# Linear attention with decay and a maxout layer: decay sums for one token of a pair, wider relus, another written order

## The chip, the cores and the metric

The kernel runs on one core of a Trainium2 chip. The metric is the device time of one execution in microseconds; a time given for a kernel is the median of its runs. Engines are named as the profile names them: PE is TensorE (PEld its weight loads), DVE is VectorE, ACT is ScalarE, POOL is GpSimd, SP is SyncE, which issues the DMAs.

## The reference

```python
# attention: q, k, v, alpha are (4, 8, 768, 48) = batch, heads, tokens, width; alpha in 0.8 .. 1.0
for t in range(S):
    state = alpha[:, :, t, :, None] * state + np.einsum('bhd,bhe->bhde', k[:, :, t], v[:, :, t])
    y[:, :, t] = np.einsum('bhd,bhde->bhe', q[:, :, t], state)
# x = y as (3072 tokens, 384); w1, w2 are (384, 1024), w_out is (1024, 384)
h1, h2 = x @ w1, x @ w2
out = np.maximum(h1, h2) @ w_out
```

Everything comes and goes as float32.

## The kernel before, in words

**The maths.** The decay recurrence is done in chunks. With L the running sum of log alpha inside a chunk, a query is multiplied by exp(L), a key by exp(-L), and inside the chunk the outputs are a masked score matrix times the values; the state (48 by 48 a head) is carried from chunk to chunk. The maxout layer is rewritten as max(h1, h2) = h2 + relu(h1 - h2): the kernel forms wd = w1 - w2 and m = w2 times w_out once, and then computes relu(x wd) w_out + x m.

**The tiling.** The tokens of a batch are cut into three blocks of 256, so there are twelve blocks n = 0 to 11, each with all eight heads. A partition holds a pair of neighbouring tokens j = 0, 1; 128 pairs make a block, and its two halves of 64 pairs are its chunks, x = 0, 1. Blocks 0 and 1 do their first steps in two halves of four heads, the others do all eight at once. Each block gives two strips of 128 output tokens, and the maxout layer takes these two strips as one group g of W = 256 tokens.

**The steps of a block** (names as in the order below, with lines of the kernel before):
- `lda`, `ldk`, `ldq`, `ldv` (L452): loads of alpha, k, q, v. One buffer of a ring of ten holds a and k, another q and v; each half of a weight matrix takes one too (`ldw1`, `ldw2`, `ldwo`).
- `ln` (L591, ACT): log of alpha, as float16. `su` (L599, DVE): the sum of the two logs of a pair.
- `cs` (PE): the decay sums. For each group of four heads one matmul of 384 columns with the constant `cmat` (L610) gives the sum up to and with the pair, written for both tokens; one of 192 columns with the negated identity (L613) takes the second token's log off again for the first token. Four small ones (L618) give the sums per head that the state needs. The result fills two PSUM banks.
- `en`, `ep` (L628, L632, ACT): exp(-sum) and exp(sum) of 768 elements. `gg` (L637): the same of the small sums.
- `kt` (L648) and `qt` (L654): key times exp(-L) and query times exp(L), float16. `vc` (L664, POOL): values to float16.
- `tk`, `tq` (L681, PE) and `ck`, `cq` (copies): transposes of keys and queries, in blocks 0 to 7. Blocks 8 to 11 transpose by DMA (`dk`, `dq`, L721).
- `kv` (L741, PE): key times value. `w` (DVE), `t32` and `T` (L788, L776, mostly POOL): the state carried on, and its float16 copy for the outputs. `g` (L754): a product of decays.
- `sc` (L821, PE): scores. `pt` (L829, DVE): scores times the mask. `yf`, `y` (L866, PE): the outputs, from state and scores. `xe`: the outputs to float16.

**The steps of a group**: `h` (L931): for each of the eight column blocks f of 128, three matmuls of 256 columns into a PSUM bank. `r` (L939 on DVE, L941 on ACT): one relu of 256 columns per f. `o` (L964): the output of a strip, eleven matmuls of 384 columns in two parts, a and b. `ev` and `st` (L973): copy to SBUF and store. `wtp`, `wtc`, `woc`, `wd`, `mp`, `mc` prepare the weights, `fill` are matmuls on zeros (L423) that keep PE busy at the start.

**What sets the order.** A planner class could choose an order from costs, but a written order (`ORDER`) stands in its place: a list of words `step:engine`, with the PSUM bank behind P. The instructions are emitted in this sequence, and each engine, SP's queue too, works off its own instructions in that sequence; a waiting instruction holds all behind it on its engine. The relevant helper reads:

```python
for word in ORDER.split():
    name, at = word.split(":")
    o = ops[name]
    o.eng = eng[at[0]]
```

Of the kernel before, what the change touches and what calls it, by code (L numbers as in the profile page):

```python
# [24 lines left out]
class Op:  # L25
    __slots__ = ("name", "engs", "emit", "deps", "takes", "uses", "prio", "mode", "xfer", "eng", "start", "end", "seen", "n", "after", "until", "port", "k")
# [5 lines left out]
GROUPS = (2, 2, 2, 2, 2, 2, 2, 2, 2, 2, 2, 2)  # L32
# [7 lines left out]
setp1:G fz:D lda0.0:S setd0:D fill0:P7 lda0.1:S fill12:P ldw21:S fill32:P fill31:P ldk0.0:S fill34:P pads1:D ldq0.0:S fill9:P ln0.0:A id32:D fill15:P  # L40
su0.0:D fill11:P ln0.1:A setd1:D ldv0.0:S fill16:P fill21:P su0.1:D mask:D cs0.0:P0 cs0.1:P ldw20:S gg0.0:A fill28:P en0.0:A pads0:D wtp1.2:P6 en0.1:A
fill8:P gg0.1:A wtp1.0:P5 ep0.0:A kt0.1:D ep0.1:A lda1.0:S fill6:P fill13:P kt0.0:G wtc1.2:A wtp1.1:P4 lda1.1:S fill3:P qt0.0:D fill14:P ldwo0:S
fill27:P tk0.0:P2 qt0.1:D tk0.1:P fill22:P ck0.0:A tq0.0:P fill36:P tq0.1:P vc0.1:G cq0.0:A fill29:P fill2:P cq0.1:D vc0.0:G fill4:P ck0.1:A ldw10:S
fill10:P wtc1.0:D pads2:G sc0.0:P0 kv0:P2 pt0.0:D fill19:P wtp0.1:P6 w0:D ldwo1:S wtp0.0:P5 ln1.0:A wtc0.1:D su1.0:D fill24:P ln1.1:A t32.1:D fill17:P
sc0.1:P0 su1.1:D fill23:P w1:D T1.0:G fill30:P wtp0.2:P6 pt0.1:D ldw11:S T1.1:G cs1.0:P2 woc0.0:G fill1:P wtc0.2:D gg1.0:A y0:P0 en1.0:A wtc0.0:D
woc0.1:A ldk1.0:S cs1.1:P mp0.1:P6 gg1.1:A wd0.0:D wtc1.1:A mp0.2:P5 ldq1.0:S xe1:A wd0.1:D mp0.0:P4 xe0:A fill7:P h0.0:P1 woc1.1:A woc1.0:D ldv1.0:S
fill20:P fill26:P g1:G fill5:P en1.1:A T2.1:G mp1.1:P ep1.0:A mp1.2:P lda2.0:S r0.0:A wd1.1:D mc1:A h0.1:P0 fill25:P h0.3:P6 wd1.0:D h0.6:P7 r0.3:A
h0.2:P1 r0.1:A mp1.0:P mc2:D kt1.0:G r0.2:A lda3.0:S h0.5:P6 r0.6:D mc0:A h0.4:P5 ldq2.0:S kt1.1:G tk1.0:P0 ep1.1:A qt1.0:D h0.7:P7 r0.4:A ck1.0:D
tq1.0:P t32.2:G r0.5:A tk1.1:P qt1.1:D o0.1a:P5 ldk2.0:S r0.7:A cq1.0:D vc1.0:G ck1.1:A tq1.1:P sc1.0:P2 vc1.1:G cq1.1:D T2.0:G kv1:P6 ldk3.0:S
o0.1b:P ln2.0:A w2:D pt1.0:D T3.1:G T3.0:G o0.0a:P4 ldv2.0:S ev0.1:A t32.3:D yf1:P0 ln3.0:A su2.0:D sc1.1:P2 o0.0b:P w3:D pt1.1:D ldq3.0:S cs2.0:P6  # L50
ev0.0:A su3.0:D y1:P lda4.0:S en2.0:A cs3.0:P2 kt2.0:G xe2:A xe3:D st0.1:S ep2.0:A h1.0:P5 st0.0:S h1.1:P4 r1.0:D gg3.0:A h1.4:P1 gg2.0:A qt2.0:D
r1.1:A g2:G ldv3.0:S h1.3:P5 T4.0:G en3.0:A h1.5:P0 h1.2:P4 vc2.0:G r1.3:D tk2.0:P6 ep3.0:A r1.2:D ldq4.0:S h1.6:P5 kt3.0:G ck2.0:D tq2.0:P r1.5:A
h1.7:P4 r1.4:A qt3.0:D o1.0a:P0 r1.7:A ldv4.0:S r1.6:A o1.1a:P1 T4.1:G cq2.0:D ln4.0:A tk3.0:P2 t32.4:G kv2:P4 ldk4.0:S sc2.0:P6 ck3.0:A tq3.0:P w4:D
pt2.0:D T5.1:G o1.1b:P cq3.0:A T5.0:G lda6.0:S su4.0:D yf2:P4 sc2.1:P6 vc3.0:G ev1.1:A sc3.1:P2 o1.0b:P pt2.1:D ldq7.0:S pt3.1:D y2:P ev1.0:A lda5.0:S
sc3.0:P0 vc4.0:G cs4.0:P6 xe4:A xe5:D pt3.0:D h2.0:P5 ldq6.0:S kv3:P2 r2.0:A h2.6:P4 en4.0:A h2.5:P5 w6:D h2.1:P1 r2.6:D T7.1:G r2.5:A h2.2:P0
ldk6.0:S T7.0:G h2.4:P4 r2.1:A r2.2:D h2.7:P5 ep4.0:A t32.7:G h2.3:P1 o2.0a:P0 kt4.0:G w7:D gg4.0:A ldv6.0:S r2.3:A r2.4:D r2.7:A qt4.0:D y3:P2
ln6.0:A lda7.0:S g4:G kv4:P4 t32.8:G xe6:A o2.0b:P su6.0:D xe7:A w8:D tk4.0:P6 st1.1:S T9.0:G ev2.0:D h3.0:P1 T8.0:G ldk5.0:S tq4.0:P ck4.0:D r3.0:A
h3.5:P0 t32.9:G cs6.0:P2 cq4.0:D r3.5:A T9.1:G h3.4:P1 ldq5.0:S w9:D T8.1:G gg6.0:A h3.3:P0 en6.0:A r3.4:D h3.7:P7 sc4.0:P4 r3.3:D h3.6:P6 kt6.0:G
ep6.0:A pt4.0:D ldv5.0:S h3.2:P1 o2.1a:P0 ln5.0:A qt6.0:D r3.7:A h3.1:P5 vc6.0:G ldv7.0:S o2.1b:P r3.1:A r3.6:A su5.0:D yf4:P2 r3.2:D ev2.1:A sc4.1:P4
cs5.0:P6 ldk7.0:S ln7.0:A pt4.1:D o3.0a:P1 en5.0:A lda9.0:S y4:P ep5.0:A kt5.0:G kv6:P4 xe8:A o3.0b:P w12:D lda8.0:S xe9:A su7.0:D o3.1a:P0 ev3.0:A  # L60
qt5.0:D t32.13:G gg5.0:A h4.0:P1 g5:G t32.10:G ldk8.0:S cs7.0:P2 w13:D r4.0:A T13.1:G h4.1:P7 en7.0:A h4.7:P6 T10.1:G h4.4:P1 r4.7:D tk5.0:P4 vc5.0:G
r4.1:A st3.0:S h4.3:P6 ep7.0:A ck5.0:D h4.5:P7 ldq9.0:S vc7.0:G o3.1b:P r4.5:A qt7.0:D T10.0:G gg7.0:A r4.4:A tq5.0:P kt7.0:G r4.3:A h4.6:P7 st2.0:S
cq5.0:D tk6.0:P2 ldq8.0:S h4.2:P6 ev3.1:D tq6.0:P r4.2:A ck6.0:D kv5:P4 g7:G sc5.0:P0 t32.14:G o4.0a:P6 r4.6:D cq6.0:A ldv8.0:S T13.0:G w10:D pt5.0:D
T11.0:G o4.1a:P7 ln9.0:A T11.1:G st1.0:S kv7:P2 ln8.0:A yf5:P0 ldv9.0:S sc5.1:P4 w14:D o4.0b:P pt5.1:D t32.15:G o4.1b:P ldk9.0:S w15:D y5:P su9.0:D
ev4.1:A su8.0:D ev4.0:D sc6.0:P2 tk7.0:P4 T15.0:G xe11:A xe10:D ldq10.0:S cs8.0:P6 T14.0:G ck7.0:A pt6.0:D h5.0:P1 vc8.0:G tq7.0:P r5.0:A h5.1:P0
lda10.0:S cq7.0:D en8.0:A h5.2:P3 h5.4:P2 r5.1:D h5.5:P1 kt8.0:G r5.4:A h5.6:P5 r5.5:D r5.2:A h5.7:P4 st2.1:S h5.3:P2 r5.6:D r5.7:A cs9.0:P0 r5.3:D
ep8.0:A sc6.1:P4 T14.1:G dk8:S o5.1a:P3 gg9.0:A qt8.0:D T15.1:G en9.0:A o5.0a:P2 lda11.0:S ep9.0:A pt6.1:D o5.1b:P gg8.0:A g8:G qt9.0:D t32.16:G
kv8:P4 ldk10.0:S ev5.1:A y6:P6 w16:D sc7.0:P0 o5.0b:P xe12:D T17.0:G xe13:A vc9.0:G pt7.0:D h6.0:P3 ev5.0:A yf7:P4 kt9.0:G sc7.1:P6 r6.0:A h6.1:P2
pt7.1:D h6.2:P3 r6.1:A h6.4:P1 ln10.0:A h6.3:P0 h6.7:P2 r6.4:D dk9:S kv9:P6 su10.0:D r6.7:A y7:P r6.2:D w18:D dq8:S cs10.0:P2 t32.19:G xe14:A xe15:D
h6.6:P1 T16.1:G r6.3:D h7.0:P5 st3.1:S w19:D r6.6:A h6.5:P4 r7.0:D en10.0:A h7.2:P0 st4.0:S h7.3:P1 h7.7:P5 r6.5:A o6.0a:P7 dq9:S r7.7:A ep10.0:A  # L70
h7.6:P6 h7.4:P5 ldv10.0:S ln11.0:A r7.6:D o6.1a:P4 r7.4:D st4.1:S gg10.0:A qt10.0:D g10:G h7.1:P6 T19.0:G h7.5:P5 r7.1:A o6.0b:P t32.20:G r7.5:D
T17.1:G r7.3:D o6.1b:P T16.0:G ev6.0:A r7.2:D kt10.0:G sc8.0:P0 ev6.1:D yf8:P2 sc8.1:P6 o7.1a:P5 pt8.1:D o7.0a:P4 T19.1:G dk10:S pt8.0:D o7.1b:P
st6.0:S su11.0:D y8:P ldk11.0:S vc10.0:G ev7.1:D ldq11.0:S sc9.0:P0 sc9.1:P6 T20.0:G xe16:D xe17:A o7.0b:P pt9.0:D h8.0:P5 dq10:S ev7.0:A cs11.0:P2
pt9.1:D r8.0:A h8.5:P4 h8.6:P5 h8.1:P1 r8.6:A h8.2:P0 r8.5:D r8.1:A kv10:P6 en11.0:A y9:P4 w20:D r8.2:D T21.1:G gg11.0:A h8.3:P1 t32.21:G xe19:D
xe18:A o8.1a:P0 kt11.0:G ep11.0:A w21:D h9.0:P7 r8.3:A h8.7:P6 h9.1:P5 r8.7:D h9.2:P4 T20.1:G r9.1:A dk11:S h9.4:P1 r9.2:D h9.7:P6 T21.0:G r9.4:A
h9.6:P5 qt11.0:D g11:G r9.7:A h8.4:P4 ldv11.0:S T22.1:G o8.0a:P1 r9.0:A r9.6:D st5.1:S r8.4:D sc10.0:P2 st5.0:S yf10:P6 sc10.1:P4 pt10.0:D o8.0b:P
o8.1b:P dq11:S pt10.1:D ev8.0:A h9.5:P1 h9.3:P3 st7.0:S o9.1a:P2 vc11.0:G st6.1:S ev8.1:A y10:P t32.22:G r9.3:A st8.1:S T22.0:G r9.5:A kv11:P4
o9.0a:P3 xe21:D xe20:A w22:D h10.0:P7 T23.0:G o9.0b:P T23.1:G r10.0:D sc11.0:P0 ev9.0:A yf11:P4 sc11.1:P6 pt11.0:D o9.1b:P st9.0:S st8.0:S h10.6:P3
pt11.1:D ev9.1:A h10.2:P1 h10.3:P0 r10.6:A st9.1:S h10.4:P2 h10.1:P3 st7.1:S r10.4:D y11:P r10.1:A r10.2:D o10.0a:P1 xe22:D xe23:A h11.0:P7 h10.5:P6
h10.7:P5 r10.5:D o10.1a:P4 r10.7:D r10.3:D h11.2:P6 o10.0b:P r11.2:A r11.0:A h11.5:P6 ev10.0:D h11.4:P7 h11.1:P5 h11.3:P3 r11.1:D h11.6:P2 h11.7:P1  # L80
r11.6:D o10.1b:P r11.7:A r11.3:D r11.5:D o11.1a:P5 ev10.1:A o11.0a:P6 r11.4:A st10.1:S o11.1b:P o11.0b:P ev11.1:A st11.1:S o11.1c:P7 ev11.0:D st10.0:S
o11.1d:P st11.0:S ev11.11:A st11.11:S
"""
SHIFT = {}
FIX = {}


class Plan:


    LAT = {"PE": 0.25, "ACT": 0.08, "DVE": 0.08, "POOL": 0.1, "SP": 0.0}
    SWITCH = 0.09
    LEAD = 4.5
# [51 lines left out]
    def give(self, b):  # L145
# [4 lines left out]
        else:  # L150
            self.free[b.pool][b.at] = True

    def add(self, name, engs, emit, deps=(), takes=(), uses=(), prio=0.0, mode=None, xfer=0.0, after=None, until=None, port=False, k=0):
        o = Op()
        o.k = 2 * k + 0.35 if k else 0
        o.until = until
        o.port = port
        prio += SHIFT.get(name, 0.0)
        if name in FIX:
            engs = {FIX[name]: engs[FIX[name]]}  # L160
# [867 lines left out]
```

## Time and profile before

| | |
|---|---|
| runs before | 143.17, 143.81, 142.78 us, median 143.17 |
| profiled execution | 142.84 us, its span 141.0 us |
| busy in the span, us | PE 133.4, PEld 96.1, DVE 92.5, ACT 74.9, POOL 65.1 |
| L610 and L613 (sums), count and mean ns | 24 of 328, 24 of 246 |
| L941 and L939 (relus of 256), count and mean ns | 55 of 383 on ACT, 41 of 419 on DVE |
| L648 (key product, 768 elements, POOL) | 10 of 1810 ns |
| loads of 384 KB, issue to landing | about 6 us |

The span is the part of the execution in which the profile sees the engines; 1.8 us of the profiled time lie outside it. Busy times of different engines overlap. A matmul's own duration holds its latency, so back-to-back matmuls overlap and the distance between their starts is what each one costs PE. The page cuts the span into 40 slices of 3.5 us and gives the busy tenths of each.

### The profile page before, as it was taken

The page shows a single profiled execution, that of the slowest core. Times are in us where ns is not written, and L with a number is a line of the kernel's source. Part 1 is how long each engine was busy: PE and PEld are TensorE (multiplying, and loading weights), DVE is VectorE, ACT ScalarE, POOL GpSimd, SP SyncE. Part 2 cuts the span into 40 slices and gives each one's busy share as a digit, 9 for nine tenths or more (in the row PEclk, how much of TensorE's full clock was granted, in tenths as well). Part 3 has the DMA queues.
Part 4 walks back from the last instruction along what each step waited for, and adds up shares of the span by engine and source line. Part 5 has one row for each costly group of instructions (what it writes and reads, how often), then busy time and mean ns, then how long its engine had stood idle before and what let it go on. Part 6 is the DMA issues. An engine that isn't in the chain of part 4 may idle for free.

```text
span 141.0 us, 5542 instructions
## 1 busy us (share of the span) xinstructions
PE 133.4 (95%) x2373; PEld 96.1 (68%) x2373; DVE 92.5 (66%) x186; ACT 74.9 (53%) x159; POOL 65.1 (46%) x108
## 2 busy tenths in 40 slices
PE   6779889989999999999999999999999999999991
PEld 2355666666877778767885976787667776777770
DVE  6615984679586976875596877873688476385420
ACT  3624267654977494876772783657205634241230
POOL 5036343652696287627994373721940742500000
PEclk9999999999999999999999999999999999999999
DMA  5999999999999999999999989397669359641014
GB/s 121 291 257 296 371 377 331 260 235 268 266 315 258 255 246 258 299 230 248 268 282 252 280 211 221 80 146 198 170 122 250 62 105 242 201 176 51 0 56 167
DMA packets 64680, 30.76 MB, mean 218 GB/s; under 512 B 58896, under 2 KB 63120, under 8 KB 64656
## 3 DMA queue, kind: packets, MB, share of 16 engines
q1 hardware_dynamic: 64656, 30.41, 85.8%
q8 instruction: 18, 0.29, 1.0%
q14 instruction: 6, 0.05, 0.1%
HBM read 23.59 MB, written 4.72 MB: 201 GB/s over the span
## 4 chain that ended last, share of the span: by engine, by line
PE 77%; SPq 10%; DMA 9%; DVE 1%; issue 1%; ACT 0%; DVEq 0%
PE PS L964 32%; PE PS L931 21%; PE PS L866 9%; DMA ldf<-in_q_dram 9%; SPq L452 6%; PE PS L681 5%; PE PS L821 4%; SPq L474 3%; PE PS L741 3%; PE PS L610 2%; SPq L471 2%; PE PS L613 1%; PE PS L618 1%; DVE xT L494 0%; DVE qkt L654 0%
## 5 line engine op out<-in xcount | busy, mean ns | idle before, releaser
L931 PE MATMUL PS<-xT,wd 128*128 128x256 f16 x288 | 37.8, 273 | 0.1
L964 PE MATMUL PS<-wo,g 128*128 128x384 f16 (+1 forms) x200 | 37.8, 320 | 0.0
L829 DVE TENSOR_TENSOR pt<-PS,mask 128x1024 f16<-128x1024 f32 x24 | 28.8, 1216 | 3.4 <-PE PS L821 3.4
L931 PEld LDWEIGHTS <-wd 128*128 128x128 f16 x288 | 26.8, 98 | 5.9 <-DVE w L801 0.4
L648 POOL TENSOR_TENSOR qkt<-ldf,en 128x768 f16<-128x768 f32 (+1 forms) x13 | 21.5, 1657 | 18.8 <-DMA ldf<-in_k_dram 10.0
L941 ACT ACTIVATE g<-PS 128x256 f16<-128x256 f32 x55 | 19.6, 383 | 16.2 <-PE PS L931 16.1
L964 PEld LDWEIGHTS <-g 128*128 128x128 f16 x200 | 18.7, 98 | 10.6
L939 DVE TENSOR_SCALAR g<-PS 128x256 f16<-128x256 f32 x41 | 16.3, 419 | 10.3 <-PE PS L931 9.5
L776 POOL TENSOR_TENSOR T<-w,gg 48x192 f16<-48x192 f32 x24 | 12.4, 518 | 12.7 <-DVE w L801 8.7
L492 ACT COPY outs<-PS 128x384 f32<-128x384 f32 (+1 forms) x18 | 8.3, 461 | 18.7 <-PE PS L964 17.2
L964 PE MATMUL PS<-m,xT 128*128 128x384 f16 (+1 forms) x75 | 15.9, 321 | 0.0
L492 ACT CAST xT<-PS 128x384 f16<-128x384 f32 x15 | 8.5, 595 | 12.1 <-PE PS L866 10.9
L664 POOL CAST v<-ldf 128x768 f16<-128x768 f32 (+1 forms) x14 | 10.2, 740 | 8.7 <-DMA ldf<-in_v_dram 8.5
L654 DVE TENSOR_TENSOR qkt<-ldf,PS 128x384 f16<-128x384 f32 x24 | 12.2, 547 | 2.5 <-DMA ldf<-in_q_dram 2.1
L423 PE MATMUL PS<-fz 128*128 128x512 f16 x34 | 11.7, 447 | 1.2 <-DVE fz L420 1.2
L591 ACT ACTIVATE loga<-ldf 128x768 f16<-128x768 f32 (+1 forms) x14 | 10.4, 750 | 4.4 <-DMA ldf<-in_alpha_dram 4.3
L681 PE MATMUL PS<-ident,qkt 128*128 128x128 f16 x128 | 10.2, 219 | 0.9 <-DVE qkt L654 0.7
L776 POOL TENSOR_TENSOR T<-w,g 48x192 f16<-48x192 f32 x16 | 8.6, 539 | 4.1 <-PE PS L866 3.5
L866 PE MATMUL PS<-pt,v 64*64 64x128 f16 x576 | 10.4, 218 | 0.0
L681 PEld LDWEIGHTS <-qkt 128*128 128x128 f16 x128 | 8.3, 98 | 2.9 <-DVE qkt L654 1.0
L628 ACT ACTIVATE en<-PS 128x768 f32<-128x768 f32 (+1 forms) x14 | 9.9, 715 | 0.4 <-POOL t L788 0.2
L632 ACT ACTIVATE PS<-PS 128x768 f32<-128x768 f32 (+1 forms) x14 | 10.0, 725 | 0.0
(73 smaller groups left out, 162.2 us busy)
## 6 DMA issues: line engine op xcount, KB each, us to landing
ldf<-in_k_dram SPq DMA_DIRECT2D x12, 384.0 KB, 6.0
ldf<-in_q_dram SPq DMA_DIRECT2D x12, 384.0 KB, 6.2
ldf<-in_v_dram SPq DMA_DIRECT2D x12, 384.0 KB, 6.0
out_dram<-outs SPq DMA_DIRECT2D x23, 192.0 KB, 3.5
ldf<-in_alpha_dram SPq DMA_DIRECT2D x10, 384.0 KB, 6.4
ldf<-in_moe_w_dram SPq DMA_DIRECT2D x4, 768.0 KB, 8.0
ldf<-in_moe_w_out_dram SPq DMA_DIRECT2D x2, 768.0 KB, 8.7
ldf<-in_alpha_dram SPq DMA_DIRECT2D x4, 192.0 KB, 4.5
```

Of the source, the lines that this page charges most:

```text
L423: plan.add(f"fill{i}", {"PE": 0.21}, lambda eng: nc.tensor.matmul(bank(fb), lhsT=fz[:, 0:128], rhs=fz, start=True, stop=True, skip_group_c ...
L492: nc.scalar.copy(out=out, in_=in_)
L648: e.tensor_mul(out=hjd(qkts[i3], 1)[:, hd], in0=A["ld", n, "k"][:, hd].rearrange("p h (j d) -> p h j d", j=2), in1=A["en", n][:, g0:g1].re ...
L654: nc.vector.tensor_mul(out=hjd(qkts[i3], 0)[:, 4 * g : 4 * g + 4], in0=A["ld", n, "q"].rearrange("p h (j d) -> p h j d", j=2)[:, 4 * g : 4 ...
L681: nc.tensor.transpose(t[:, a, r, j, :], src[:, j, r, :], ident16)
L776: e.tensor_mul(out=T16s[m % 4][o : o + 48, :, 48 * u : 48 * u + 48], in0=w_[o : o + 48], in1=g_[o : o + 48])
L829: nc.vector.tensor_mul(out=t.rearrange("p u r c -> p (u r) c"), in0=A["sc", n, hf].rearrange("p u (r c) -> p (u r) c", r=2), in1=mask.rear ...
L866: nc.tensor.matmul(dst, lhsT=lhsT, rhs=rhs, start=(x, u) not in begun, stop=done and ends[x, u] == i, skip_group_check=True)
L931: nc.tensor.matmul(t[:, 0:W], lhsT=wd16[:, s, f * 128 : (f + 1) * 128], rhs=xT[:, s, a0 : a0 + W], start=(s == 0), stop=(s == 2))
L939: nc.vector.tensor_relu(o, i)
L941: nc.scalar.activation(out=o, in_=i, func=ACTF.Relu)
L964: nc.tensor.matmul(A["op", t0, c], lhsT=lhsT, rhs=rhs, start=(part == 0 and j == 0), stop=(part == 1 and j + 1 == len(todo[1])))
```

## The change

- The sums are made for the second token of a pair only: one matmul of 384 columns with `cmat` per block, one PSUM bank. The negated identity is gone. `en` and `ep` take 384 elements, and `kt` and `qt` read them once for each token of the pair.
- The first token is put right beforehand: its key is multiplied by the second token's alpha (`ka`), its query by exp(-log alpha) of the second token (`inv` on ACT, then `qi`). Both work in place in the load buffer.
- Two column blocks f share a PSUM bank, and one relu takes 512 columns: 48 `h` steps of six matmuls, 48 `r` steps. The first part of an output takes three matmuls with x and four with g (three before), the second four (five before).
- `su`, `kt`, `vc`, `T` and `t32` may be put on other engines. In the new order: `su` 10 on POOL and 4 on DVE (14 on DVE before), full and half `kt` 7 on DVE and 7 on POOL (1 and 13), `vc` 11 on ACT and 3 on POOL (14 on POOL), `T` 10 on DVE and 30 on POOL (40 on POOL), `ka` 6 on DVE and 8 on POOL, `qi` 4 and 10, `fill` 41 (34).
- The written order is another one on every queue.

The core of the diff:

```diff
-                for g in gs:
-                    nc.tensor.matmul(t[:, g, 0:384], lhsT=cmat,
-                                     rhs=s16[:, 4 * g : 4 * g + 4, 0:D].unsqueeze(2).to_broadcast([128, 4, 2, D]),
-                                     start=True, stop=False, skip_group_check=True)
-                    nc.tensor.matmul(t[:, g, 0:384].rearrange("p (h j d) -> p h j d", h=4, j=2)[:, :, 0, :], lhsT=nid16,
-                                     rhs=l1[:, 4 * g : 4 * g + 4, :], start=False, stop=True, skip_group_check=True)
+                t, s16 = A["cs", n], s16s[i2]
+                nc.tensor.matmul(t[:, h0 * D : h1 * D].rearrange("p (h d) -> p h d", d=D), lhsT=cmat, rhs=s16[:, h0:h1, 0:D],
+                                 start=True, stop=True, skip_group_check=True)
...
+                nc.scalar.activation(out=A["inv", n][:, hd], in_=A["loga", n][:, hd, 1, :], func=ACTF.Exp, scale=-1.0)
...
+                kk = A["ld", n, "k"][:, hd, 0:D]
+                e.tensor_mul(out=kk, in0=kk, in1=A["ld", n, "a"][:, hd, D : 2 * D])
...
+                qq = A["ld", n, "q"][:, hd, 0:D]
+                e.tensor_mul(out=qq, in0=qq, in1=A["inv", n][:, hd])
...
-            kt = plan.add(f"kt{n}.{i}", ke, e_kt, deps=[en, lk[0], pads[i3]] + free3, uses=[bk, enb], prio=Q + 6, port=True)
+            kt = plan.add(f"kt{n}.{i}", ke, e_kt, deps=[en, ka, lk[0], pads[i3]] + free3, uses=[bk, enb], prio=Q + 6, port=True)
...
-                t = A["h", g, f] = bank(ps, WMAX)
-                for s in range(3):
-                    nc.tensor.matmul(t[:, 0:W], lhsT=wd16[:, s, f * 128 : (f + 1) * 128], rhs=xT[:, s, a0 : a0 + W],
-                                     start=(s == 0), stop=(s == 2))
+                t = A["h", g, f] = bank(ps, 2 * W).rearrange("p (f w) -> p f w", f=2)
+                for i in range(2):
+                    for s in range(3):
+                        nc.tensor.matmul(t[:, i], lhsT=wd16[:, s, (f + i) * 128 : (f + i + 1) * 128], rhs=xT[:, s, a0 : a0 + W],
+                                         start=(s == 0), stop=(s == 2), skip_group_check=True)
...
-                o, i = A["g16", g][:, f, 0:W], A["h", g, f][:, 0:W]
+                o, i = A["g16", g][:, f : f + 2], A["h", g, f]
...
-                    todo = [gw[:4], xm + gw[4:]] if early else [xm + gw[:3], gw[3:]]
+                    todo = [gw[:4], xm + gw[4:]] if early else [xm + gw[:4], gw[4:]]
```

The stretch of the order around blocks 1 and 2 that the prediction walks through, the words of PE alone. Before:

```
h0.0 fill20 fill26 fill5 mp1.1 mp1.2 h0.1 fill25 h0.3 h0.6 h0.2 mp1.0 h0.5 h0.4 tk1.0 h0.7 tq1.0 tk1.1 o0.1a tq1.1 sc1.0 kv1 o0.1b o0.0a yf1 sc1.1 o0.0b cs2.0 y1 cs3.0 h1.0
```

After:

```
h0.0 mp1.1 mp1.2 mp1.0 h0.2 h0.4 h0.6 o0.0a tk1.0 o0.0b kv1 tk1.1 tq1.0 fill33 tq1.1 fill35 fill38 fill11 sc1.0 o0.1a yf1 sc1.1 cs2.0 o0.1b y1 cs3.0 tk2.0 h1.0
```

The loads on SP's queue, before: a0, half of w2, k0, q0, v0, half of w2, a1, half of wo, half of w1, the other halves of wo and w1, k1, q1, v1, a2, a3, q2, k2, k3, v2, q3, a4. After: a0, half of w2, half of a1, k0, q0, the rest of a1, half of w2, v0, half of wo, half of w1, the other halves of wo and w1, q1, k1, v1, a2, k2, a3, q2, q3, k3, v2, v3, a4. The planner's costs for the new steps and engines, which the written order leaves unused, are left out here.

## The prediction

> **What bounds the kernel now.** I read the page first, for which engine is full and when.
>
> ```profile
> PE 133.4 (95%) x2373; PEld 96.1 (68%) x2373; DVE 92.5 (66%) x186; ACT 74.9 (53%) x159; POOL 65.1 (46%) x108
> ...
> PE   6779889989999999999999999999999999999991
> ```
>
> TensorE has holes in the first ten slices (35 us) only. PE's waits name them all, and they add up to 4.5 us:
>
> ```profile
> PE PS L511 <- DMA ldf<-in_moe_w_dram: 2.0, 2, 1.6
> PE PS L423 <- DVE fz L420: 1.2, 1, 1.2
> PE PS L681 <- DVE qkt L654: 0.7, 1, 0.7
> PE PS L866 <- DVE pt L829: 0.4, 1, 0.4
> PE PS L681 <- POOL qkt L648: 0.2, 1, 0.2
> ```
>
> Then the chain of waits from 28 us on (start, length, what), because a busy PE need not be at its rate.
>
> ```profile
> 15.68 12.45 DMA ldf<-in_q_dram
> ...
> 28.83 0.71 PE PS L681 x8
> ...
> 34.66 0.16 PE PS L610
> 34.82 0.08 PE PS L613
> 34.91 0.16 PE PS L610
> 35.07 0.08 PE PS L613
> 35.15 0.08 PE PS L618 x4
> ...
> 36.93 2.16 PE PS L931 x18
> ...
> 58.06 0.35 PE PS L821 x16
> ...
> 61.57 0.22 PE PS L821 x16
> ...
> 133.65 4.43 PE PS L964 x38
> 138.08 0.02 issue
> 138.10 0.32 ACT outs L492
> ```
>
> Until 28.1 us the kernel waits for the queries of block 1; from 36.93 to 138.08 us the chain is PE and nothing else. Of the excess over each group's best rate, nearly all sits at switches between full-array matmuls and 64-wide ones: sixteen score matmuls take 0.22 us after others of their kind and 0.35 behind full-array ones; the output stage behind them begins some 0.1 late as well. So in these 101 us a matmul removed is time removed, and so is a switch (about 0.11 us). The last view is busy time by stretch (us, PE, PEld, DVE, ACT, POOL ...):
>
> ```profile
> 40.00:60.00 20.00, 20.00 (x430) 15.09 (x428) 15.50 (x28) 13.55 (x27) 13.30 (x20) 1.00 1.10 271
> 60.00:80.00 20.00, 20.00 (x432) 14.84 (x431) 14.16 (x28) 12.97 (x25) 13.02 (x20) 1.00 1.03 259
> ```
>
> The other engines are 65 to 78% full; their idle time there mostly waits for PE.
>
> **The Trainium skill.** "TensorE: Matmul & The Clock Gate", Back-to-back issue gap: N/2.4 + 2.5 ns, for 384 columns 162 ns. The chain shows 0.16; the 328 ns of the groups by form is latency, not a price. "TensorEngine Tiling (Array Packing)", Key Properties: changing the tiling mode drains TensorE; the 0.11 us agree. "SBUF — State Buffer", on the shared port pair: a VectorE operation with two SBUF inputs and a GpSimd one that reads SBUF exclude each other for a whole instruction. The trace agrees: one half-width key product on POOL took 1.34 us beside VectorE's other half (9.39 to 9.95 us), the other two 1.0.
>
> **The change part by part.** Its sum is made against the profiled execution, 142.84 us, 1.84 of it outside the span of 141.0; the median of the runs is 143.17.
>
> (1) Removed, decay sums. A full block had two L610 of 384 columns (0.16 each) and two L613 of 192 (0.08 each); it keeps one of 384. That is 0.48 - 0.16 = 0.32 to 0.33 us. Blocks 0 to 3 have theirs before 36.93 us, where loads set the time, so I count blocks 4 to 11 only: 8 x 0.33 = **-2.6 us**. The four others would be 1.3 us if loads were no cover.
>
> (2) Switches. In the two written orders, from the first output of block 1 to the end, the changes between the two kinds of matmul fall from 45 to 41: 4 x 0.11 = **-0.4 us**.
>
> (3) The head. Block 0, six weights and block 1 are loaded ahead of everything else in both orders, so block 1's last values should land at 29.5 us as now. Inside it, queries and keys swap: queries at 26.0, keys at 28.15. Behind them block 2's keys now go before block 3's alpha, which landed at 32.66 and will at about 34.3 (one load is some 1.65). Walk, with today's durations: DVE scales half the keys (0.3) and multiplies by the decay (0.56), so `tk1.0`, at the head of PE's queue, starts at 29.1. PE has been idle since about 27.7. `o0.0b` behind it, ready all that time, runs to 30.5. `kv1` waits for two casts on ACT (29.55 + 2 x 0.5) and starts at 30.7. Transposes and four fills, which are lost time there, end at 32.7; `cq1.0`, on DVE behind seven other steps, is done at 32.45, so the scores start at 32.75 (30.41 now). But `o0.0` is done already, so `y1` starts at 36.0 against 35.16. Behind it: alpha of block 3 at 34.3, Ln 0.85, two Exp of 384 at 0.49, `kt2.0` on DVE 0.96, `xe3` 0.6: the first matmul of group 1 starts at 37.85 instead of 36.93: **+0.9 us**. Ahead of it now stands `tk2.0`, eight transposes that came later before: **-0.45 us**. Bounds: no loss if keys land as early as today (0), twice that if the queue also slips by a load (+1.8); I take the walk.
>
> (4) Two column blocks per bank: 288 matmuls as before, so nothing on PE. Relus: 96 become 48. ACT takes 383 ns for 256; its groups grow by 0.85 ns a column (491 at 384, 819 at 768), so 0.60 for 512; DVE 419 ns and 1.06 a column (its output copies take 555 at 384), 0.69. That frees some 8 us of the two engines. A group gets its first half after 12 matmuls instead of 4 relus of 3 each, the same. Nothing on the path; without cover, the last relu of a group is 0.2 to 0.27 us later, and 7 matmuls of the output (1.1 us) cover it.
>
> (5) Added: per block an Exp of 384 (0.49), a key and a query scaling of 384 float32. On DVE these are 0.56 (half-width key product, same size), on POOL 1.0. Removed: half of two Exps (0.81 to 0.49), and a query product of 2 x 0.55 becomes one of about 0.96. I counted the orders for blocks 2 to 9 and priced them with these rows. POOL: 26 T at 0.52, 8 products at 1.81, 10 t32 at 0.51, 8 casts at 0.83, 5 g: 41 us; after: 20 T, 6 products, 7 t32, 2 casts, 5 g and 18 half-width steps (6 keys, 7 queries, 5 sums): 46. ACT 51 to 53. DVE 59 to 59. PE needs 68 for these blocks. So all stays under PE: 0, if the strict queues are met. I allow 0.2 for small waits.
>
> (6) Loads from block 4 on: same bytes in another order; 6.4 us per block (four of 1.6) against 8 of PE. Nothing. The eight transposing DMAs and the 25 stores keep their kinds; between each pair of transposes and its scores lie several us of PE work.
>
> Sum: -2.6 - 0.4 + 0.9 - 0.45 + 0.2 = -2.35; 142.84 becomes **140.5 us**. For the median of runs, 0.3 above the profiled one before, I keep 140.5, since runs scatter by 1.0.
>
> **The rivals.**
> - The head costs nothing: keys in time, fills harmless. For: both orders load the same bytes before 29.5. Against: `tk1.0` blocks a ready `o0.0b`. Time: 140.5 - 0.9 = 139.6.
> - Fuller side engines give part back: queues are in order, so a late scaling on POOL delays the key product, the transpose and PE. For: POOL gains 5 us of work in 68, and POOL's query scalings of blocks 2 and 3 stand ahead of a key product and wait for loads. Against: some 7 us of PE work stand between most such pairs. With 0.2 us at each of 8 blocks: +1.6, so 142.1 (141.2 to 143.5).
> - Slower: the port pair. In blocks 2 to 9 DVE gets 17 operations with two SBUF inputs (six T, three t32, three scalings, two key products, three sums; before, eight sums), each of which can be held by a running POOL operation of 0.5 to 1.8 us. DVE has 68 - 59 = 9 us of slack, so at 0.5 us each it is as full as PE; to be 1% slower than now PE must lose another 4 us, at 0.75 us each. Against: POOL is busy two thirds of the time with ops of mean 0.8, so a wait of 0.3 is likelier, and today's DVE sums take 0.37. At 0.75 us the time is 140.5 + 17 x 0.75 - 9 = 144.3, at 0.8 us 145: I write 145 us.
> - The sums don't come off PE (something else takes the slots, idle for lack of loads): the DMA share is 1.0 to 1.1 until 78 us. Time: 143.
>
> **How the numbers follow.** The sum as it stands (own range 139.9 to 141.3) 0.48; a free head 0.14; fuller side engines 0.25; port pair 0.09; nothing gained 0.04. A measurement of this kernel tells about 1% (1.4 us) from no change. Faster, below 141.7: 0.48 + 0.14 + 0.09 of the third. Same: 0.15 of the third, 0.04, and 0.01 of the port pair. Slower: the rest, 0.09 with rounding. The range runs from 139.1, just under the free head, to 142.9, which leaves out a tail of the third case and the port pair.
>
> **What would show it.** Right: the 384-column sums 14 instead of 24 and no negated-identity matmul; the first matmul of group 1 at 37 to 38 us; from there to the end of PE about 98 us without named waits; relus at 0.60 and 0.69. Wrong: PE waits of over 1 us after 40 us, on a key product or scaling (side engines) or on the masked scores with DVE above 85% (port pair); or a stretch of PE no shorter than 101 us.

## The result and the profile after

The changed kernel takes 141.65 us (median of 141.05 to 141.92), the kernel before beside it 143.21 us (142.78 to 143.81): a ratio of 0.988, 95% interval 0.983 to 0.993. The prediction was 140.5 us with a range of 139.1 to 142.9. The profiled execution after took 141.61 us, its span 139.8. Medians here and below are of all runs of a kernel; the ratios leave out runs of over 1.5% above its fastest one.

In three of the profiles used below (no late fills, second order of the head, wide relus alone) the granted clock averaged 0.988. In each it was 0.50 for one stretch of 3.4 us between 8 and 15 us, ahead of everything that is compared here, and 1.00 from there to PE's end.

The page after, busy times and TensorE's slices:

```profile
PE 131.8 (94%) x2346; PEld 93.7 (67%) x2346; DVE 100.2 (72%) x164; ACT 80.5 (58%) x163; POOL 67.7 (48%) x109
...
PE   6959996998999999999999999999999999999991
```

PE's waits, the four longest:

```profile
PE PS L419 <- DVE fz L416: 1.2, 1, 1.2
PE PS L605 <- ACT en L640: 1.1, 1, 1.1
PE PS L532 <- ACT wo L488: 1.1, 1, 1.1
PE PS L692 <- DVE qk L490: 0.5, 1, 0.5
```

And the chain of waits from 25 us on (start, length, what). Lines after the change: L624 is `ka`, L661 `kt`, L629 `qi`, L692 transposes, L419 fills, L832 scores, L605 decay sums, L877 outputs, L943 `h`, L976 `o`.

```profile
15.57 12.70 DMA ldf<-in_k_dram
28.30 0.37 DVE ldf L624
28.69 0.56 DVE qkt L661
...
30.32 0.66 DVE ldf L629
...
32.24 0.44 DVE qk L490
32.72 0.38 PE PS L692 x4
33.10 0.65 PE PS L419 x3
33.75 0.35 PE PS L832 x16
...
36.88 0.96 PE PS L877 x60
...
38.66 2.71 PE PS L943 x24
...
133.30 3.62 PE PS L976 x33
```

The shape is the old one: loads first, then PE alone. Only the joint between the two has changed. It is now a string of short DVE steps behind block 1's keys, and group 1 starts at 38.66 us where it started at 36.93. From there PE needs 136.91 - 38.66 = 98.25 us to its end; before it was 138.08 - 36.93 = 101.15. So the span's 1.2 us are +1.73 in the head and -2.90 behind it.

The two stretches that were shown of before:

```profile
40.00:60.00 20.00, 19.81 (x432) 15.39 (x430) 16.61 (x26) 16.18 (x31) 14.90 (x22) 1.00 1.15 264
60.00:80.00 20.00, 19.87 (x428) 14.72 (x426) 17.28 (x26) 14.17 (x30) 15.53 (x21) 1.00 1.04 263
```

PE has lost 0.2 and 0.1 us there, although DVE, ACT and POOL are all fuller, DVE up to 86%. Over the whole stretch from 40 us to the end it is some 0.45 us of new idle time.

### The profile page after: what moved, and what is told of

It reads as the page before. It is cut to its first block, busy times and chain, and to the rows that moved or that the text cites. A ratio compares the mean times of both kernels' runs of the same rounds, so it can differ in the third digit from the quotient of the medians.

```text
span 139.8 us, 5453 instructions
## 1 busy us (share of the span) xinstructions
PE 131.8 (94%) x2346; PEld 93.7 (67%) x2346; DVE 100.2 (72%) x164; ACT 80.5 (58%) x163; POOL 67.7 (48%) x109
## 4 chain that ended last, share of the span: by engine, by line
PE 73%; SPq 10%; DMA 9%; DVE 4%; issue 1%; ACT 1%; DVEq 0%
PE PS L976 31%; PE PS L943 21%; PE PS L877 9%; DMA ldf<-in_k_dram 9%; SPq L448 6%; PE PS L692 4%; PE PS L832 4%; SPq L467 3%; SPq L470 2%; PE PS L752 2%; PE PS L605 1%; DVE qk L490 1%; DVE w L812 1%; DVE ldf L629 0%; PE PS L419 0%
## 5 line engine op out<-in xcount | busy, mean ns | idle before, releaser
L976 PE MATMUL PS<-wo,g 128*128 128x384 f16 (+1 forms) x200 | 37.7, 320 | 0.0
L943 PE MATMUL PS<-xT,wd 128*128 128x256 f16 x288 | 35.9, 273 | 0.3 <-ACT xT L488 0.2
L943 PEld LDWEIGHTS <-wd 128*128 128x128 f16 x288 | 27.3, 98 | 5.4 <-DVE xT L490 0.6
L953 ACT ACTIVATE g<-PS 128x512 f16<-128x512 f32 x32 | 18.8, 598 | 13.0 <-PE PS L943 12.7
L976 PEld LDWEIGHTS <-g 128*128 128x128 f16 x200 | 18.6, 98 | 10.8
L787 POOL TENSOR_TENSOR T<-w,gg 48x192 f16<-48x192 f32 x17 | 9.4, 553 | 16.1 <-DVE w L812 9.8
L629 POOL TENSOR_TENSOR ldf<-ldf,inv 128x384 f32<-128x384 f32 (+1 forms) x10 | 9.8, 983 | 15.2 <-DMA ldf<-in_q_dram 13.3
L661 POOL TENSOR_TENSOR qkt<-ldf,en 128x768 f16<-128x768 f32 (+1 forms) x7 | 11.9, 1698 | 10.7 <-DVE ldf L624 8.5
L976 PE MATMUL PS<-m,xT 128*128 128x384 f16 (+1 forms) x75 | 15.8, 320 | 0.0
L419 PE MATMUL PS<-fz 128*128 128x512 f16 x41 | 13.3, 451 | 1.2 <-DVE fz L416 1.2
L951 DVE TENSOR_SCALAR g<-PS 128x512 f16<-128x512 f32 x16 | 10.9, 686 | 3.3 <-PE PS L943 3.2
L666 DVE TENSOR_TENSOR qkt<-ldf,PS 128x768 f16<-128x768 f32 (+1 forms) x14 | 11.6, 834 | 2.4 <-ACT PS L644 2.2
L692 PE MATMUL PS<-ident,qkt 128*128 128x128 f16 x128 | 10.3, 219 | 1.0 <-DVE qk L490 0.5
L692 PEld LDWEIGHTS <-qkt 128*128 128x128 f16 x128 | 8.2, 97 | 3.5 <-issue 1.0
L877 PE MATMUL PS<-pt,v 64*64 64x128 f16 x576 | 10.2, 218 | 0.0
L596 POOL TENSOR_TENSOR s<-loga 128x384 f16<-128x384 f16 (+1 forms) x10 | 7.9, 799 | 4.4 <-ACT loga L588 4.2
L488 ACT COPY qk<-PS 128x1024 f16<-128x1024 f16 (+1 forms) x11 | 9.0, 820 | 1.8 <-PE PS L692 1.6
L488 ACT CAST v<-ldf 128x768 f16<-128x768 f32 (+1 forms) x11 | 8.1, 742 | 3.0 <-DMA ldf<-in_v_dram 3.0
```

The lines of the kernel that those rows point to most:

```text
L419: plan.add(f"fill{i}", {"PE": 0.21}, lambda eng: nc.tensor.matmul(bank(fb), lhsT=fz[:, 0:128], rhs=fz, start=True, stop=True, skip_group_c ...
L488: nc.scalar.copy(out=out, in_=in_)
L661: e.tensor_mul(out=hjd(qkts[i3], 1)[:, hd], in0=A["ld", n, "k"][:, hd].rearrange("p h (j d) -> p h j d", j=2), in1=f.unsqueeze(2).to_broad ...
L666: nc.vector.tensor_mul(out=hjd(qkts[i3], 0)[:, hd], in0=A["ld", n, "q"][:, hd].rearrange("p h (j d) -> p h j d", j=2), in1=f.unsqueeze(2). ...
L692: nc.tensor.transpose(t[:, a, r, j, :], src[:, j, r, :], ident16)
L877: nc.tensor.matmul(dst, lhsT=lhsT, rhs=rhs, start=(x, u) not in begun, stop=done and ends[x, u] == i, skip_group_check=True)
```

## The experiments

**What was in doubt.** Theory P is the prediction's walk: PE's strict queue costs the head its time, with a ready output (`o0.0b`) behind the late `tk1.0` and four fills as lost work. Theory D: DVE's line of steps behind the landing of block 1's keys sets the head, whatever PE does meanwhile. Behind the head, the question is whether the removed sums and the switches are what shortened PE's stretch, and what the new order has to do with it (theory Q: without the refitted order and engines the columns don't come off).

The runs scatter by about 1 us, and the traces show a cause: block 1's keys land anywhere from 27.0 to 29.5 us. So I measure from the first key scaling of block 1 (`ka1.0`) to three points: the first score-times-value matmul of block 1 (`y1`), the first `h` of group 1, PE's end. The changed kernel has 8.50, 10.27 and 108.61 us. In a second trace of it the first two repeat to 0.01 us and the third to 0.26 us, so a difference of 0.3 us at PE's end says little. The starts are those of the timeline, some 0.08 us ahead of the chain's.

In all but two of these kernels the key scaling starts 0.02 or 0.03 us behind the keys' landing. In the second and third order of the head it starts 0.69 and 0.57 us behind it, so their rows in the table flatter them; the numbers from the landing stand with those two runs.

| kernel | median us | ratio to before (95%) | to `y1` | to group 1 | to PE's end |
|---|---|---|---|---|---|
| changed kernel | 141.65 | 0.988 (0.983 to 0.993) | 8.50 | 10.27 | 108.61 |
| again, unedited | 141.60 | 0.988 (0.985 to 0.990) | 8.51 | 10.27 | 108.87 |
| no late fills | 141.69 | 0.988 (0.984 to 0.991) | 8.51 | 10.27 | 108.64 |
| ready output first | 141.86 | 0.989 (0.985 to 0.993) | 8.98 | 10.74 | 109.23 |
| a sum on POOL, no fills | 141.57 | 0.986 (0.983 to 0.990) | 7.87 | 9.91 | 108.73 |
| head, first order | 142.05 | 0.991 (0.987 to 0.994) | 8.19 | 9.95 | 108.28 |
| head, second order | 141.35 | 0.982 (0.976 to 0.988) | 7.51 | 9.29 | 107.72 |
| head, third order | 141.97 | 0.990 (0.987 to 0.993) | 6.75 | 8.92 | 109.32 |
| sums paid again | 143.77 | 1.001 (0.999 to 1.004) | 8.52 | 10.28 | 111.01 |
| twenty more switches | 143.29 | 1.002 (0.999 to 1.005) | 8.51 | 10.27 | 110.31 |

**No late fills.**

```diff
- fill33:P fill35:P fill38:P fill11:P
```

> The changed kernel without its four late fills (fill33, fill35, fill38, fill11). In the changed kernel the outputs of block 1 (y1) start at 36.88 us and group 1 at 38.66. Theory D (the head's delay is DVE's queue: from 28.3 us DVE runs sixteen steps without a pause until the second masked scores of block 1 end at 36.75): the scores move up to about 33.1, but DVE takes the mask only at about 34.4, so y1 stays at 36.9 within 0.15 and the time at 141.6. Theory P (TensorE's own queue, as my walk had it: fills are lost time): y1 at 36.2, time 141.0.

Nothing moved by more than 0.03 us. The fills stand on the chain of waits, and yet they cost nothing, because the masks on DVE come later anyway. P loses half of its loss.

**The ready output first.**

```diff
- tk1.0:P0 ... o0.0b:P
+ o0.0b:P tk1.0:P0
```

> The changed kernel with the ready output half o0.0b ahead of the key transposes tk1.0. Theory P (TensorE idles while ready work stands behind tk1.0): up to 1.1 us earlier, y1 at about 36.0. Theory D: the transposes start about 0.8 later (30.1), the key copy on DVE with them, and all that is behind it; y1 later by 0.4 to 0.5, at 37.3, time 142.0.

The head became 0.48 us longer, as D said. The output delays the transpose, and the string of steps behind it is the one that counts. P's other half falls too.

**A sum on POOL, no fills.** The timeline of the changed kernel shows what holds DVE's line the longest: `su2.0` (start, length, engine, line):

```profile
32.70 1.52 DVE L596 TENSOR_TENSOR s<-loga 128x384 f16<-128x384 f16 x1
...
33.02 0.99 POOL L624 TENSOR_TENSOR ldf<-ldf 128x384 f32<-128x384 f32 x1
```

The sum took 0.37 us before. Here it spans the end of a `T` on POOL (32.55 to 33.05) and the whole key scaling behind it, and is done 0.2 us after that (34.22 against 34.01), as the prediction's port pair would have it. Both masks of block 1 wait behind it on DVE.

```diff
- su2.0:D          (behind the transposes' copies)
+ su2.0:G          (ahead of ka2.0:G), four fills dropped
```

> The changed kernel without the four late fills and with the pair sum of block 2 on POOL ahead of its key scaling instead of on DVE, where it took 1.52 us in the trace (0.37 in the kernel before). Theory D: DVE is free for the mask 1.2 us earlier, at about 33.3, y1 at 35.9 to 36.1, group 1 at about 37.8, time 140.8. Theory P: only the fills count, y1 at 36.2 as in the run without fills, and no more from the sum. If neither is the cause: 36.9 and 141.6.

`y1` came 0.63 us earlier (0.8 to 1.0 expected). Then `kt2.0` on DVE was held in its turn (1.72 us for 1.00), group 1 kept 0.36, and the end nothing (+0.1); the median is 141.57 us where 140.8 was expected. The move shows that this step held the head. That the port pair is what stretched it rests on the times of the lines above.

**The head in three other orders.** The first puts the query scaling ahead of the key's landing and the sum of block 2 ahead of the query copy; the second gives both query scalings and the sum to POOL, does transposes of queries before the keys come, and leaves DVE only the four key steps; the third moves one word more.

```diff
# second order, the words that matter
+ qi1.0:G qi1.1:G ... qt1.0:D qt1.1:D o0.0a:P6 tq1.0:P tq1.1:P cq1.0:A ka1.0:D kt1.0:D ka1.1:D kt1.1:D ... su2.0:G
# third order
- su2.0:G cs2.0:P6 yf1:P0 sc1.1:P2 pt1.1:D
+ su2.0:G yf1:P0 sc1.1:P2 cs2.0:P6 pt1.1:D
```

> The changed kernel with its head rearranged after theory D: the query scaling qi1.0 runs before the keys land, while DVE is idle; the pair sum of block 2 ahead of the last query copy, before POOL starts its key scaling; no late fills; one output half ahead of the last transposes; the sums and negative Exp of block 2 earlier. From the first key scaling of block 1 to the start of group 1 the changed kernel takes 10.3 us. Theory D: 1.2 to 1.6 us less, about 8.9, and the time 140.3. If the head's delay has another cause (loads, TensorE's queue): over 9.9 us, and the time within 0.4 of 141.6.

> The changed kernel with another order of its head, made after the last run showed a chain that goes from the keys' landing over the second half's key product on POOL to key times value: query scalings on POOL while it is idle, queries multiplied, transposed and copied (by ACT) before the keys land, all four key steps on DVE in one row, the pair sum of block 2 on POOL, no late fills. Counted from the first key scaling of block 1: y1 starts 8.5 us behind it in the changed kernel. If the head's delay is the sum of these short steps (theory D widened to DVE, POOL and ACT): 7.0 us, group 1 at 8.8 instead of 10.3, TensorE's end 1.2 to 1.5 us nearer to the keys (108.6 now), time 140.3. If loads alone set it: no change from 8.5, 141.6.

> The second order of the head with one word moved: the decay sums of block 2 (cs2.0) stand behind the second scores of block 1 on PE's queue instead of ahead of the state outputs and those scores. Theory D (the head's time is set by whatever stands in line behind block 1's key): the masked scores of the second half no longer wait 0.84 us, so from the first key scaling of block 1 to y1 it takes 6.7 to 6.9 us (7.51 with the second order, 8.50 in the changed kernel), to the first matmul of group 1 8.7 (9.29; 10.27) if block 2's key product keeps its place behind y1, and to PE's end 107.2 (107.72; 108.61); the median some 140.9 us. Rival (block 2's sums set it): the exponentials and the key product of block 2 come later by the same 0.5 to 0.8 us, so group 1 still starts 9.3 after the first scaling and the time is that of the second order, 141.35 us.

First order: 0.3 us, where 1.4 were expected. Another string took over at once: the half key product on POOL (1.00), a log on ACT (0.85), the sum, the copy, the scores.

Second: by the table 1.0 us to `y1` and to group 1 and 0.9 to the end, where 1.5, 1.5 and 1.2 to 1.5 were expected. Most of that comes from the point that it is counted from. DVE now does both query products first, and the key scaling stands right behind them, without a wait for its load:

```profile
28.78 1.10 DVE L659 TENSOR_TENSOR qkt<-ldf,PS 128x384 f16<-128x384 f32 x2 [0.48 <-POOL ldf L622]
...
29.80 0.35 DVE L617 TENSOR_TENSOR ldf<-ldf 128x192 f32<-128x192 f32 x1
```

The keys had landed at 29.11. From the landing the second order takes 8.20 us to `y1`, 9.98 to group 1 and 108.41 to PE's end, where the changed kernel takes 8.52, 10.29 and 108.63: a gain of 0.3, 0.3 and 0.2 us. A stall of 0.84 us is left in it (the second mask waits for scores that stand behind `cs2.0`).

Third: that stall went, and by the table `y1` comes at 6.75, as expected. From the landing it is 7.32 to `y1` and 9.49 to group 1, so 1.2 and 0.8 us of the head did go. But the end came 1.6 us later than in the second order, where 0.5 us earlier was expected. PE's waits after 36 us, and the chain there:

```profile
PE PS L745 <- DVE qkt L654: 0.9, 1, 0.9
PE PS L685 <- DVE qkt L659: 0.8, 1, 0.8
PE PS L598 <- POOL s L589: 0.4, 1, 0.4
```

```profile
32.32 7.39 DMA ldf<-in_k_dram
...
40.32 0.96 DVE qkt L659
...
41.32 0.62 PE PS L685 x8
```

Block 3's keys land at 39.71, 10.9 us after the first scaling. DVE waits 1.2 us for them, with block 2's query product behind their scaling in its queue, and PE waits for that product. In the changed kernel, where group 1 is later, they land at 39.16 and no wait for them shows. The second wait is on block 6's keys, issued at 57.72 (56.08 in the changed kernel); what held its buffer was not followed. So up to 0.8 us of the way to group 1 can be taken out, but it comes back as a wait for loads. At PE's end no order of the head gained more than some 0.3 us, about the scatter of that number.

> The changed kernel once more, unedited, on the same chip as the third order of the head, so that the two can be set beside each other. All theories: 8.5 us from the first key scaling of block 1 to y1, 10.27 to the first matmul of group 1, 108.6 to PE's end; the median 141.6 us, give or take 0.3.

It repeated: 8.51, 10.27, 108.87, and 141.60 us. The second order's median (141.35) is the lowest of all versions; against the changed kernel's its interval is too wide to call it faster.

**Sums paid again.** Blocks 4 to 11 repeat a matmul of 384 columns and two of 192 into the same places; nothing else changes.

```diff
  nc.tensor.matmul(... lhsT=cmat, rhs=s16[:, h0:h1, 0:D] ...)
+ if n >= 4:  # the same matmul of 384 columns again, and two of 192
```

> The changed kernel with the columns that it removed paid again in blocks 4 to 11: one more matmul of 384 columns and two of 192 per block, into the same places with the same values. The prediction's first step (a decay-sum column removed after the head is time removed, 0.33 us a block): 8 x 0.33 = 2.6 us more, span 142.4, time 144.2. If the side engines had become the bound there: under 1 us more, since TensorE would fill idle time.

To PE's end it took +2.40 us (expected 2.64; 2.14 against the second trace of the changed kernel), and the time is that of before, ratio 1.001. The chain shows each repeated matmul at its price:

```profile
57.66 0.16 PE PS L605
57.82 0.16 PE PS L608
57.98 0.17 PE PS L611 x2
```

So 0.27 to 0.30 us a block, and the removed sums account for what the change gains.

**Twenty more switches.** Ten score or key-value steps of blocks 4 to 11 were moved between two outputs or `h` steps (74 changes of kind in the whole order where the changed one has 54; the 41 of the prediction are counted from `y1` on).

```diff
- o2.0a ... (sc4.0 beside its kind)
+ o2.0a sc4.0      (and nine more)
```

> The changed kernel with ten small score or key-times-value steps moved behind one neighbouring full-array step each, so that TensorE changes between full-array and 64-wide matmuls 74 instead of 54 times with the same matmuls. The prediction's step 2 (0.11 us a switch): 20 x 0.11 = 2.2 us more from the first key scaling of block 1 to TensorE's end, 110.8 instead of 108.6, time 143.8. If switches are free: 108.6 and 141.6, save for a later mask or two.

+1.70 us to the end (expected 2.2), 0.085 each; against the second trace of the changed kernel 1.44 and 0.07.

**Parts alone, in the order of before.** Three kernels keep the old written order as far as they can: the wide relus without the new sums; the new sums without the wide relus; both, with the value casts moved to ACT.

```diff
# wide relus alone: before, with paired h and r
- h1.0 h1.1 ... r1.0 r1.1
+ h1.0 ... r1.0
# sums alone: before, relus of 256, scalings on POOL
+ inv:A behind ln, ka ahead of kt, qi:G behind kt
# both: as sums alone, with wide relus
- vc2.0:G ... vc11.0:G
+ vc2.0:A ... vc11.0:A
```

> The kernel before with the wide relus alone: two column blocks per bank, 48 relus of 512 columns, each pair at the place in the old order where its first half stood; the rest as before. The prediction's step 4 (nothing on the path, TensorE does the same columns and had no idle time after 36.9 us): same time as before within 0.4 us, although DVE and ACT are some 8 us less busy together. If relus or banks held TensorE back unseen: 1 us or more faster.

> The changed decay sums alone (one matmul per block, key and query scaled beforehand), relus of 256, in the order of the kernel before; the new scalings stand beside the products that need them, on POOL from block 2 on, and casts, products and state copies stay on POOL. By the sum alone: -2.6 us on TensorE after the head, about 0.7 more in the head, so 141.5. Theory Q (the side engines had to be rearranged for the sums to come off): POOL has about 7.2 us of work per block where TensorE needs 8.2, in a strict queue, so TensorE waits for products or state copies several times and the time is 142.5 to 145.

> Both parts of the change (sums, wide relus) in the order of the kernel before, with the value casts of blocks 2 to 11 moved from POOL to ACT, the scalings as in the run of the sums alone. POOL falls to about 6.4 us per block. By the sum alone 141.5; theory Q: better than the sums alone on a full POOL by a good part of what those lost, but still waits on POOL; 141.5 to 143.

Wide relus alone: 150.75 us, ratio 1.047 (1.043 to 1.052). Sums alone: 154.77, 1.079 (1.075 to 1.083). Both: 153.44, 1.067 (1.062 to 1.072). All three miss what was expected of them by 7 us and more.

The first loses PE time in a few places, 0.8 us at 53 where an output waits for a relu, 1.6 at 125 where block 11's values, issued late behind a transposing DMA, are cast on POOL. In all PE is idle for 4.5 us in it from group 1 on, and group 1 starts 0.7 later; the other 2 us of its span are not found. The second leaves PE idle for 9.3 us from 37 us to its end. One stretch, and the chain ahead of it:

```profile
40.00:60.00 20.00, 16.36 (x375) 11.85 (x373) 12.59 (x19) 10.64 (x22) 14.09 (x19) 1.00 1.14 266
```

```profile
40.16 0.82 POOL v L489
40.98 0.96 POOL ldf L621
...
42.02 1.81 POOL qkt L658
43.83 0.97 POOL ldf L626
```

POOL is only 70% busy in this stretch, but cast, key scaling, key product and query scaling stand in one line, 4.6 us long, and the scores come behind them. The new order has casts on ACT, half of the key products on DVE, and scalings on either. With the casts moved and the relus wide (third kernel) PE has 17.00 of these 20 us, 0.64 more. So the old order doesn't carry the change, nor either part of it. That POOL is the reason, as theory Q has it, is shown for this stretch only: the wide relus alone add nothing to POOL and lose 4.7%, and the third kernel changes two things at once.

## Why the prediction was right, and where it was not

The time came out 1.15 us above the point that was predicted and inside the range. The range was wide enough to hold the rival of fuller side engines (142.1) as well, so the median alone doesn't tell which account is right; the steps do. Of the signs named, the stretch behind the head (98.25 us, no wait of over 0.2), the relu times and the 14 sums came (ten of 384 columns, and four of 192 for the half blocks, which the prediction counted as 384 too). Group 1 at 37 to 38 us did not: it started at 38.66.

**The term that was mis-sized: step (3), the head.** Predicted +0.9, measured +1.73; 0.15 of it is that the load landed later in this execution (28.28 against 28.13). The walk's first half is good: `cq1.0` done at 32.45 (32.66 in the trace), and `y1` to group 1 takes 1.78 us (1.85). What failed is "the scores start at 32.75 ... `y1` starts at 36.0": the scores came at 33.7, behind `tq1.1`'s transposes and the fills, and `y1` at 36.88. Neither of the causes that the walk named was at work; the first two experiments show it. What was missing was the price of DVE's line when POOL works beside it: the query scaling `qi1.0` takes 0.73 us beside POOL's half key product, where the other one takes 0.35, and `su2.0` 1.52 for 0.37:

```profile
27.44 0.35 DVE L629 TENSOR_TENSOR ldf<-ldf,inv 128x192 f32<-128x192 f32 x1
...
29.75 1.00 POOL L661 TENSOR_TENSOR qkt<-ldf,en 128x384 f16<-128x384 f32 x1 [8.53 <-DVE ldf L624]
...
30.24 0.73 DVE L629 TENSOR_TENSOR ldf<-ldf,inv 128x192 f32<-128x192 f32 x1
```

Of these only the second was tested by itself (0.63 us to `y1`); the other orders of the head show that several strings of nearly equal length lie there, since each repair handed the path to the next. The 0.9 was thus the right kind of loss, put down to the wrong engine's queue; that its sign and order of size came out is in part luck.

**Step (1), the sums:** -2.6 predicted; the repeat says 2.1 to 2.4. The step stands.

**Step (2), the switches:** -0.4 predicted at 0.11 each; at the 0.07 to 0.085 measured it is some -0.3. The -0.45 for `tk2.0` was not tested by itself; eight transposes do stand ahead of group 1 in the chain and take 0.47.

**Step (4), wide relus:** predicted 0.60 and 0.69 us. The groups by form (count, busy, mean ns):

```profile
L953 ACT ACTIVATE g<-PS 128x512 f16<-128x512 f32 x32 | 18.8, 598 | 13.0 <-PE PS L943 12.7
L951 DVE TENSOR_SCALAR g<-PS 128x512 f16<-128x512 f32 x16 | 10.9, 686 | 3.3 <-PE PS L943 3.2
```

A line through two sizes of the same engine gave the third. "Nothing on the path" fits the new order, where PE shows no named wait for a relu, though no run takes the wide relus out of it; in the old order they cost some 7 us. The prediction did not say that its zero hung on the order.

**Step (5), side engines:** 0.2 us allowed, 0.45 of idle time found, none of it a named wait of over 0.2. The sum behind the head then is -2.40 - 0.34 - 0.45 + 0.45 = -2.74 against -2.90 measured, within the 0.26 us by which PE's end repeats.

**Step (6), loads:** nothing, as predicted; but the third order shows how near they are: a group 1 that comes 0.8 us sooner behind the keys meets them.

**The port pair (rival)** is real as an effect: the full-width `su` on DVE, before and after:

```profile
L599 DVE TENSOR_TENSOR s<-loga 128x384 f16<-128x384 f16 x10 | 3.6, 372 | 0.1
```

```profile
L596 DVE TENSOR_TENSOR s<-loga 128x384 f16<-128x384 f16 x3 | 3.0, 988 | 0.0
```

It is not the bound after 40 us: PE's only named wait there is 0.2 us, on a cast of ACT's. Where it did act is the head, the one place where DVE had no slack, and there the prediction did not look for it. "Nothing gained" falls with the repeated sums.

## What to carry to other kernels

Work taken off the full engine is worth its issue price, by the count, as long as the rest can be refitted around it; parts of the same edit, and both together, lost 7 to 12 us in an order made for other durations. When a stretch ends in a string of short steps on one engine, price each step as it runs beside its neighbours, and expect that the second longest string is a few tenths behind. A filler shown on the chain of waits needn't cost anything: take it out before blaming it. And a stretch that is compared between versions has to start at an event that the edit can't move, such as a landing.

## What the runs showed of the hardware

- One load sequence, issued in the same order, landed block 1's keys between 27.0 and 29.5 us in the ten traces of the changed kernel and its variants. Of the changed kernel's two traces and the one without late fills, the spans are 139.8, 139.1 and 140.0 us and the landings 28.3, 27.3 and 28.4: from the landing on they agree within 0.3 us.
- In the two kernels with the old order and new sums TensorE's granted clock fell to 0.50 for one stretch of 3.4 us (68.8 to 72.2 us with the sums alone, 70.3 to 73.7 with both; 0.91 in the mean from 60 to 80), though PE's longest single wait was 1.9 us. The Trainium skill, "TensorE: Matmul & The Clock Gate", Part 1: The HAM clock gate, has the clock fall after an idle window of about 3.4 us; no such window shows here. What the traces show is that in the 3.4 us ahead of the fall PE was busy for 1.55 and 1.76 us, so about half of the time, while stretches of that length with 1.86 and 1.91 us (sums alone) were followed by the full clock. With 1.74 (twenty more switches) and 1.78 us (wide relus alone) it stayed full too, so about half busy is the border as far as these traces tell; no run was made to test it. The fall is part of the loss of these two kernels.
